# Products of w3 and w_out spread over steps 0 to 3 of a banded attention, and a feed-forward that begins with a whole pair of chunks

## Chip, core and metric

One core of one Trainium2 chip. The metric is the device time of one execution in microseconds (us). Engines: TensorE (PE; its weight loads are shown as PEld), VectorE (DVE), ScalarE (ACT), GpSimd (POOL, nearly unused here) and SyncE (SP), which issues all DMAs.

## The reference

Attention with a band of 96 keys and 8 global keys and a linear bias by distance, 4 batches, 8 heads, 768 tokens, head size 64; its output, as 3072 tokens by 512, goes through a gated feed-forward without a nonlinearity:

```python
scores = scale * np.matmul(q, k.transpose(0, 1, 3, 2)) + bias      # kept: 8 global keys, 96 local ones
a = softmax(np.where(keep, scores, -1e9))
x = np.matmul(a, v)            # 3072 x 512
a = x @ w1                     # 512 x 1024
b = x @ w2                     # 512 x 1024
h = a * b @ w3                 # 1024 x 1024
return h @ w_out               # 1024 x 512
```

The four weights are float64.

## The kernel before

**Attention in steps.** The tokens are cut into 12 chunks of 256. A step does two pairs of heads of one chunk, so a chunk takes 2 steps and there are 24. Step s has four parts. `visit(s)` does the products with v of step s - 1 on PE (L468), the scores of step s (L405), and, on ACT and DVE, the merging of the products with v into the chunk's x, which is split into a high and a low part, `xh` and `xl` (L503, L504, L63, L64). `all_rows(s)` adds the bias and takes the maximum on DVE (L420) and the exponential on ACT (L421). The scaling by the sums is on ACT (L433), from step 4 on half of it on DVE (L435). `turn(s, i)` transposes the probabilities of head pair i on PE (L445, L447), and ACT copies them out of PSUM as `ph` (L449). The transposes and the products with v share two PSUM buffers (pool `ps_v`).

**Feed-forward.** w3 and w_out are multiplied into one matrix first, so that the rest is (x w1 * x w2) (w3 w_out). `fold(f, k)` is one product of that, a float32 matmul of 128x128 by 128x512 (L142, two instructions in the trace), eight of them for each of eight blocks f of d_ff; after the eighth, ACT copies the block's high part `wh` out of PSUM (L144), and `low(f)` makes its low part on DVE (L147), which also frees the PSUM buffer. `run` is the feed-forward proper, with three matmuls for each product (high by high, high by low, low by high: L161 to L163, L178 to L180). For each f it makes `m` for w1 and for w2 in PSUM, copies the first to `a` (ACT, L168), multiplies on DVE (`g`, L171) and splits the result into `gh` and `gl`. The `m` tiles have two PSUM buffers, which folds use too. `run` works on 512 columns (a pair of chunks) or on 256 (one chunk). It yields after every 6 matmuls of 512 columns, or 12 of 256; `slices(k)` runs k of these pieces, and `SLICES` says how many go between the parts of a step. A pair is 48 pieces, 32 of products with w1 and w2 and 16 of output.

**Weights.** `weights` fetches a piece of float64 (512 KB) into a staging buffer by a DMA on SP's queue and makes float32 of it with three integer instructions on DVE (`convert`, L54, L56, L58). `w3(f)` does the two pieces of block f of w3, `w12(f)` the pieces of w1 and w2 of block f, which land in `t3s`; ACT then makes the high part (L122) and DVE, by `lows()`, the low one (L130). The staging buffers are four `stage` slots and two `raws` slots; a DMA into one waits until DVE has converted what was there.

**Order.** PE runs in the order of the program throughout. In `first_steps` DVE and SP do so as well, while ACT's instructions are put in order by a scheduler; later all engines but PE are scheduled, and ACT and DVE carry out their instructions in the order that results. `first_steps` interleaves the conversions, the 64 folds and the first steps of attention. In the kernel before it covers steps 0 to 3. Chunks 0 and 1 have feed-forwards of their own, of 256 columns, and that of chunk 0 begins in step 3.

## Time and profile before

| | |
|---|---|
| time, median of 3 runs | 591.76 us (591.63 to 592.16) |
| profiled execution: time, span | 591.84 us, 589.8 us |
| PE, DVE, ACT busy in the span | 565.4 us (96%), 274.2 us (46%), 297.3 us (50%) |
| mean granted clock of PE | 0.993 |

The span is the time from the first to the last instruction; the execution has 2.0 us more around it. "Busy" is the time in which an engine carried out at least one instruction. Matmuls overlap, so the distance between the starts of two of them is what one costs, and the duration of a single one is longer.

### The profile page before, as it was taken

To read this page: it belongs to the slowest core of one execution; us is meant where nothing else is said; L and a number is where in the kernel's file an instruction comes from. 1 tells how busy PE (TensorE), PEld (TensorE's weight loads), DVE (VectorE), ACT (ScalarE), POOL (GpSimd) and SP (SyncE) were. 2 spreads that over 40 slices of the span, in tenths; PEclk is the share of its full clock that TensorE was granted. 3 is DMA by queue.
4 is the path that set the end of the run, shared out by engine and by line. 5 is a ranking of instruction groups with operands and counts; after the bars stand their busy time and mean duration, and the time that the engine had idled before them with its cause. 6 is when DMAs were issued, how large, how long until landed. Compare 5 with 4: busy or idle time off the path is not lost.

```text
span 589.8 us, 12652 instructions
## 1 busy us (share of the span) xinstructions
PE 565.4 (96%) x5216; PEld 452.0 (77%) x5216; DVE 274.2 (46%) x875; ACT 297.3 (50%) x801; POOL 1.3 (0%) x10
## 2 busy tenths in 40 slices
PE   2998996999999999999999999999999999999995
PEld 0444556989988888888888888888888888888884
DVE  8999999524444445404534432552244354022200
ACT  3065688446666456536646545663555565322210
POOL 0000000000000000000000000000000000000000
PEclk9999997999999999999999999999999999999999
DMA  8896754202223202212210330221232020100001
GB/s 300 306 359 239 224 217 148 82 21 82 65 80 116 67 15 81 64 55 82 81 57 24 102 114 18 66 64 35 82 116 79 2 82 1 54 19 1 0 36 41
DMA packets 23252, 54.19 MB, mean 92 GB/s; under 512 B 2705, under 2 KB 4753, under 8 KB 23185
## 3 DMA queue, kind: packets, MB, share of 16 engines
q1 hardware_dynamic: 23184, 53.29, 26.6%
q8 instruction: 43, 0.70, 0.5%
q14 instruction: 25, 0.20, 0.1%
HBM read 46.99 MB, written 6.29 MB: 90 GB/s over the span
## 4 chain that ended last, share of the span: by engine, by line
PE 82%; DVE 13%; ACT 2%; DMA 2%; issue 1%; DVEq 0%; ACTq 0%
PE m L161 15%; PE m L162 15%; PE m L163 15%; PE o L178 8%; PE o L179 7%; PE o L180 7%; PE v L468 5%; PE s L405 4%; PE t L445 3%; PE t L447 3%; DVE pr L420 2%; DVE t L58 1%; DVE t L56 1%; DVE t3s L56 1%; DMA stage<-w3t 1%; DVE t3s L58 1%
## 5 line engine op out<-in xcount | busy, mean ns | idle before, releaser
L421 ACT ACTIVATE pr<-pr,mx 128x232 f32<-128x232 f32 (+1 forms) x192 | 88.3, 461 | 23.4 <-DVE mx L420 21.6
L171 DVE TENSOR_TENSOR g<-m,a 128x512 f32<-128x512 f32 x48 | 33.0, 687 | 132.0 <-PE m L163 128.6
L161 PE MATMUL m<-xh,w2h 128*128 128x512 f32 (+1 forms) x224 | 84.4, 377 | 0.0
L161 PE MATMUL m<-xh,w1h 128*128 128x512 f32 (+1 forms) x224 | 81.6, 364 | 0.0
L162 PE MATMUL m<-xl,w1h 128*128 128x512 f32 (+1 forms) x224 | 81.0, 362 | 0.0
L163 PE MATMUL m<-xh,w1l 128*128 128x512 f32 (+1 forms) x224 | 81.0, 361 | 0.0
L162 PE MATMUL m<-xl,w2h 128*128 128x512 f32 (+1 forms) x224 | 80.8, 361 | 0.0
L163 PE MATMUL m<-xh,w2l 128*128 128x512 f32 (+1 forms) x224 | 80.7, 360 | 0.0
L178 PE MATMUL o<-wh,gh 128*128 128x512 f32 x192 | 77.0, 401 | 0.0
L179 PE MATMUL o<-wl,gh 128*128 128x512 f32 x192 | 75.1, 391 | 0.0
L180 PE MATMUL o<-wh,gl 128*128 128x512 f32 x192 | 74.9, 390 | 0.0
L142 PE MATMUL w<-wo,t 128*128 128x512 f32 x128 | 60.6, 623 | 13.1 <-DVE wo L58 11.1
L449 ACT ACTIVATE ph<-t 128x512 f32<-128x512 f32 (+1 forms) x96 | 49.8, 557 | 44.2 <-PE t L447 29.5
L504 DVE TENSOR_TENSOR vs<-v,vs 128x512 f32<-128x512 f32 x24 | 16.6, 690 | 117.2 <-ACT vs L503 117.2
L63 ACT ACTIVATE gh<-g 128x512 fp32r<-128x512 f32 x48 | 30.3, 630 | 68.1 <-DVE g L171 68.1
L142 PEld LDWEIGHTS w<-wo,t 128*128 128x128 f32 x128 | 24.3, 198 | 42.5 <-issue 24.2
L420 DVE CUSTOM_DVE_ANT_0 pr<-s,biasw 128x232 f32<-128x232 f32 x160 | 54.9, 394 | 0.0
L168 ACT ACTIVATE a<-m 128x512 f32<-128x512 f32 x48 | 28.4, 591 | 45.0 <-PE m L163 45.0
L161 PEld LDWEIGHTS m<-xh,w2h 128*128 128x128 f32 x224 | 42.3, 189 | 8.7 <-issue 2.6
L161 PEld LDWEIGHTS m<-xh,w1h 128*128 128x128 f32 x224 | 43.0, 192 | 6.6 <-DVE t3s L58 0.2
L445 PE MATMUL t<-ident,pr 128*128 128x128 f32 x192 | 43.0, 278 | 5.3 <-ACT pr L433 5.2
L162 PEld LDWEIGHTS m<-xl,w1h 128*128 128x128 f32 x224 | 43.0, 192 | 6.4
(84 smaller groups left out, 800.5 us busy)
## 6 DMA issues: line engine op xcount, KB each, us to landing
qr<-qk SPq DMA_DIRECT2D x32, 312.0 KB, 4.4
vr<-vx SPq DMA_DIRECT2D x32, 256.0 KB, 3.5
stage<-w3t SPq DMA_DIRECT2D x15, 512.0 KB, 6.8
out_dram<-ot SPq DMA_DIRECT2D x24, 256.0 KB, 2.0
raws<-w SPq DMA_DIRECT2D x10, 512.0 KB, 6.1
qr<-qk SPq DMA_DIRECT2D x16, 260.0 KB, 4.1
vr<-vx SPq DMA_DIRECT2D x16, 192.0 KB, 3.7
stage<-w SPq DMA_DIRECT2D x6, 512.0 KB, 7.1
```

The costliest lines, as they stand in the source:

```text
L142: nc.tensor.matmul(ps, lhsT=self.t3[f, z][:, i * P:(i + 1) * P].bitcast(F32), rhs=self.wo[:, k].bitcast(F32), start=k == 0, stop=k == NFC - 1)
L161: nc.tensor.matmul(ps[:, z], lhsT=mh, rhs=xh[:, i], start=i == 0, stop=False)
L162: nc.tensor.matmul(ps[:, z], lhsT=mh, rhs=xl[:, i], start=False, stop=False)
L163: nc.tensor.matmul(ps[:, z], lhsT=ml, rhs=xh[:, i], start=False, stop=i == NCC - 1)
L171: nc.vector.tensor_tensor(out=g, in0=ps, in1=a, op=ALU.mult)
L178: nc.tensor.matmul(ps, lhsT=gh[:, f, ts], rhs=self.wh[:, f], start=f == 0, stop=False)
L179: nc.tensor.matmul(ps, lhsT=gh[:, f, ts], rhs=self.wl[:, f], start=False, stop=False)
L180: nc.tensor.matmul(ps, lhsT=gl[:, f, ts], rhs=self.wh[:, f], start=False, stop=f == NFC - 1)
L420: nc.vector.tensor_tensor_reduce(out=pr[:, j, u, w0:], in0=ps[u][:, j, w0:UW], in1=bias, scale=-SCALE, scalar=3.0e38, op0=ALU.add, op1=ALU ...
L421: nc.scalar.activation(pr[:, j, u, w0:], pr[:, j, u, w0:], AF.Exp, bias=m, scale=-1.0, accum_out=sm[:, j, u:u + 1])
L445: nc.tensor.transpose(pt[:, u, 0], pr[:, j, u, BW:UW], ident)
L449: nc.scalar.activation(ph[:, :, :nk], pt[:, :, :nk], AF.Copy)
```

## The change

The folds of blocks 3 to 7 are no longer done in one go between the parts of steps 0 to 2. `around` puts a few of them before, between and after the two turns of steps 0 to 3. `first_steps` covers step 4 too. The feed-forward of 256 columns is gone: the first `run` is that of chunks 0 and 1 together, it begins in step 4, after `visit(4)`, and gets 10 pieces there and 12 in each step after it. `low(2)` moves ahead of `w3(4)`. The conversions of w1 and w2 move back: block 0 comes as two single pieces after the rows of step 1, block 1 in step 2, blocks 2 and 3 in step 3, blocks 4 to 7 in step 4. Blocks 2, 4 and 5 go through `stage` slots, blocks 0, 1, 3, 6 and 7 through `raws` (before: 3, 5, 6 and 0, 1, 2, 4, 7). From step 8 on the program is the same; at its start both kernels have 46 of the first 48 pieces behind them.

```diff
--- before.py
+++ after.py
@@ -102,7 +102,7 @@
             if kind == "w":
                 f, n = divmod(at[0], 2)
 
-                raw = self.stage[{3: 0, 5: 2, 6: 0}[f] + n] if f in (3, 5, 6) else self.raws[:, n]
+                raw = self.stage[{2: 0, 4: 2, 5: 0}[f] + n] if f in (2, 4, 5) else self.raws[:, n]
                 dst, src = self.t3s[:, at[0] % 4], self.src[n][f]
                 fresh.append((n, f, dst.bitcast(F32).rearrange("p (i m) -> p i m", i=NCC)))
             elif kind == "o":
@@ -503,9 +503,7 @@
             nc.scalar.activation(v, uu[1], AF.Copy)
             nc.vector.tensor_tensor(out=v, in0=uu[0], in1=v, op=ALU.add)
             split(nc, *(x[:, h0:h0 + STEP] for x in xc), v)
-            if h0 + STEP == NP and c < 2:
-                work.append(ff.run(c, *xc, c * T, T))
-            elif h0 + STEP == NP and c % 2:
+            if h0 + STEP == NP and c % 2:
                 work.append(ff.run(c, *x2, (c - 1) * T, W))
         return ps
 
@@ -561,68 +559,75 @@
                 softmax(*p, *r, nc.scalar)
             loads(s + 1)
 
-        def fold_and_turn(f, s):
-            ff.fold(f, 0, 1, 2, 3)
-            turn(s, 0, prs)
-            ff.fold(f, 4, 5, 6)
-            turn(s, 1, prs)
-            ff.fold(f, 7)
+        def around(s, a, b, e):
+
+            for i, part in enumerate((a, b, e)):
+                for f, k0, k1 in part:
+                    ff.fold(f, *range(k0, k1 + 1))
+                if i < STEP:
+                    turn(s, i, prs)
 
         w3(3)
         scale(0)
         ff.low(0)
+        ff.low(2)
         w3(4)
         ff.low(1)
-        ff.low(2)
+        around(0, [(3, 0, 1)], [(3, 2, 2)], [(3, 3, 4)])
         w3(5)
-        w12(0)
-        fold_and_turn(3, 0)
+        prs = all_rows(1, visit(1))
+        ff.fold(3, 5, 6, 7)
+        ff.weights(("w", 0))
+        ff.low(3)
+        scale(1)
+        ff.weights(("w", 1))
+        around(1, [(4, 0, 4)], [(4, 5, 5)], [(4, 6, 7)])
         ff.lows()
         w3(6)
-        prs = all_rows(1, visit(1))
-        ff.low(3)
-        ff.fold(4, *range(NFC))
+        prs = all_rows(2, visit(2))
+        ff.low(4)
+        scale(2)
         w12(1)
-        scale(1)
-        ff.lows()
+        around(2, [(5, 0, 7), (6, 0, 0)], [(6, 1, 1)], [(6, 2, 3)])
+        ff.lows()
+        ff.low(5)
         w3(7)
-        ff.low(4)
-        fold_and_turn(5, 1)
         w12(2)
-        ff.lows()
-        ff.low(5)
-        prs = all_rows(2, visit(2))
-        ff.fold(6, *range(NFC))
+        prs = all_rows(3, visit(3))
+        ff.lows()
+        scale(3)
         w12(3)
-        scale(2)
+        around(3, [(6, 4, 7), (7, 0, 3)], [(7, 4, 5)], [(7, 6, 7)])
         ff.lows()
         ff.low(6)
-        fold_and_turn(7, 2)
         w12(4)
         ff.lows()
+        ff.low(7)
+        prs = all_rows(4, visit(4))
         w12(5)
-        ff.lows()
-        ff.low(7)
-        prs = all_rows(3, visit(3))
+        slices(2)
+        scale(4)
+        ff.lows()
+        slices(SLICES[0] - 2)
         w12(6)
+        turn(4, 0, prs)
         slices(2)
-        scale(3)
-        ff.lows()
+        ff.lows()
+        slices(SLICES[1] - 2)
         w12(7)
-        slices(SLICES[3][0] - 2)
-        ff.lows()
-        for i in range(STEP):
-            turn(3, i, prs)
-            slices(SLICES[3][i + 1])
+        turn(4, 1, prs)
+
+        slices(SLICES[2] - 2)
+        ff.lows()
         fits(nc, ff.mp, nf, oki)
 
 
-    SLICES = [()] * 3 + [(4, 4, 2)] * 3 + [(4, 2, 2)] * 2 + [(5, 4, 3)] * (n - 8)
+    SLICES = (5, 4, 3)
     with tc.manual_schedule(engines={mybir.EngineType.PE}):
         with tc.manual_schedule(engines={mybir.EngineType.DVE, mybir.EngineType.SP}):
             first_steps()
         with tc.manual_schedule(engines={mybir.EngineType.Activation}):
-            for s in range(4, n + 1):
+            for s in range(5, n + 1):
                 rs = all_rows(s, visit(s))
                 if s == n:
                     break
@@ -631,10 +636,10 @@
                 for p, r in zip(pairs(s), rs):
                     softmax(*p, *r, nc.vector)
                 loads(s + 1)
-                slices(SLICES[s][0] - 2)
+                slices(SLICES[0] - 2)
                 for i in range(STEP):
                     turn(s, i, rs)
-                    slices(SLICES[s][i + 1])
+                    slices(SLICES[i + 1])
             slices(10 ** 6)
```

Three places show what this does to the order. The names carry the head pair of the chunk and a buffer number. First, ACT in step 1. Before, its order after the exponentials of step 1 was:

```order
L144 ACTIVATE wh<-w_486 128x512
L122 ACTIVATE w1h<-t3s 128x512
L122 ACTIVATE w2h<-t3s 128x512
L433 ACTIVATE pr_2_463<-pr_2_463,sm_2_465 128x128 x2
L433 ACTIVATE pr_2_463<-pr_2_463,sm_2_465 128x232 x2
L433 ACTIVATE pr_3_474<-pr_3_474,sm_3_476 128x128 x2
L433 ACTIVATE pr_3_474<-pr_3_474,sm_3_476 128x232 x2
```

Now it is:

```order
L144 ACTIVATE wh<-w_340 128x512
L122 ACTIVATE w1h<-t3s 128x512
L433 ACTIVATE pr_2_437<-pr_2_437,sm_2_439 128x128 x2
L433 ACTIVATE pr_2_437<-pr_2_437,sm_2_439 128x232 x2
L433 ACTIVATE pr_3_448<-pr_3_448,sm_3_450 128x128 x2
L433 ACTIVATE pr_3_448<-pr_3_448,sm_3_450 128x232 x2
L449 ACTIVATE ph_2_0_504<-t_2_0_501 128x2x128
L449 ACTIVATE ph_2_1_511<-t_2_1_506 128x512
L449 ACTIVATE ph_3_0_517<-t_3_0_514 128x2x128
L449 ACTIVATE ph_3_1_524<-t_3_1_519 128x512
L122 ACTIVATE w2h<-t3s 128x512
L144 ACTIVATE wh<-w_495 128x512
```

The high part of w2's block, `w2h`, stood ahead of the scaling and now stands behind the copies of both turns.

Second, DVE around the conversion of the last block of w1 and w2. Before (the two rows at the top end that conversion, and the last row begins the merging of step 3's products with v):

```order
L56 SCALAR_TENSOR_TENSOR t3s<-raws,t3s 128x512 x2
L58 SCALAR_TENSOR_TENSOR t3s<-raws,t3s 128x512 x2
L171 TENSOR_TENSOR g_0_958<-m_0_1_933,a_0_899 128x512
L64 TENSOR_TENSOR gl_873<-g_0_958,gh_872 128x512
L130 TENSOR_TENSOR w1l<-t3s,w1h 128x512
L130 TENSOR_TENSOR w2l<-t3s,w2h 128x512
L171 TENSOR_TENSOR g_2_1030<-m_2_1_1005,a_2_1003 128x512
L64 TENSOR_TENSOR gl_873<-g_2_1030,gh_872 128x512
L319 TENSOR_SCALAR okt<-nf 128x1 x6
L320 TENSOR_REDUCE okt<-okt 128x1
L321 CAST oki<-okt 128x1
L504 TENSOR_TENSOR vs_2_1153<-v_1_2_1087,vs_2_1153 128x512
```

Now (from the split of the first `g` of step 4 to the merging of step 4's products with v):

```order
L64 TENSOR_TENSOR gl_1002<-g_0_1053,gh_1001 128x512
L54 TENSOR_SCALAR t3s<-raws 128x512 x2
L56 SCALAR_TENSOR_TENSOR t3s<-raws,t3s 128x512 x2
L58 SCALAR_TENSOR_TENSOR t3s<-raws,t3s 128x512 x2
L130 TENSOR_TENSOR w1l<-t3s,w1h 128x512
L130 TENSOR_TENSOR w2l<-t3s,w2h 128x512
L171 TENSOR_TENSOR g_1_1111<-m_1_1_1096,a_1_1094 128x512
L64 TENSOR_TENSOR gl_1002<-g_1_1111,gh_1001 128x512
L54 TENSOR_SCALAR t3s<-raws 128x512 x2
L56 SCALAR_TENSOR_TENSOR t3s<-raws,t3s 128x512 x2
L58 SCALAR_TENSOR_TENSOR t3s<-raws,t3s 128x512 x2
L504 TENSOR_TENSOR vs_0_1236<-v_2_0_1170,vs_0_1236 128x512
```

Blocks 6 and 7 now follow each other and both come through `raws`, and the merging that opens the next step's work stands straight behind block 7.

Third, SP's queue with the semaphores that each DMA waits for, at the last fetches of w1 and w2. Before:

```order
L383 DMA qr_0_913<-qk 128x624 [waits DMAHW7_49,PE_49]
L383 DMA qr_1_915<-qk 128x624 [waits DMAHW0_49,PE_49]
L390 DMA vr_0_917<-vx 128x512 [waits DMAHW1_49]
L390 DMA vr_1_919<-vx 128x512 [waits DMAHW2_49]
L50 DMA raws<-w 128x1024 [waits DMAHW3_49,DVE_49]
L50 DMA raws<-w 128x1024 [waits DMAHW4_49,DVE_49]
L390 DMA vr_2_1225<-vx 128x512 [waits DMAHW5_49,PE_49]
```

Now:

```order
L383 DMA qr_2_1030<-qk 128x624 [waits DMAHW1_49,PE_49]
L383 DMA qr_3_1032<-qk 128x624 [waits DMAHW2_49,PE_49]
L390 DMA vr_2_1034<-vx 128x512 [waits DMAHW3_49]
L390 DMA vr_3_1036<-vx 128x512 [waits DMAHW4_49]
L50 DMA raws<-w 128x1024 [waits DMAHW5_49,DVE_49]
L50 DMA raws<-w 128x1024 [waits DMAHW6_49,DVE_49]
L50 DMA raws<-w 128x1024 [waits DMAHW7_49,DMAHW5_49,DVE_49]
L50 DMA raws<-w 128x1024 [waits DMAHW6_49,DMAHW0_49,DVE_49]
L390 DMA vr_0_1296<-vx 128x384 [waits DMAHW1_49,PE_49]
```

The last two `raws` rows are block 7; their DVE semaphore is that of block 6's conversion, which empties the two slots.

## Rows read from the trace of the kernel before

**Rows 1.** The page: the busy time of each engine, and two rows of the span in 40 equal slices of 14.7 us (busy share in tenths; PEclk is the granted clock of TensorE in tenths of full speed).

```profile
PE 565.4 (96%) x5216; PEld 452.0 (77%) x5216; DVE 274.2 (46%) x875; ACT 297.3 (50%) x801; POOL 1.3 (0%) x10
...
PE   2998996999999999999999999999999999999995
...
PEclk9999997999999999999999999999999999999999
```

**Rows 2.** Windows of the span: stretch, its length, then busy us (and instructions) of PE, PEld, DVE, ACT, POOL; granted clock; DMA share; GB/s.

```profile
40.00:88.00 48.00, 45.84 (x436) 24.30 (x435) 45.62 (x115) 30.71 (x81) 0.00 (x0) 1.00 0.68 242
...
114.00:180.00 66.00, 65.96 (x786) 60.55 (x789) 28.70 (x116) 39.64 (x117) 0.00 (x0) 1.00 0.24 74
180.00:517.00 337.00, 337.00 (x3367) 279.20 (x3360) 131.96 (x481) 184.15 (x497) 0.00 (x0) 1.00 0.20 63
```

**Rows 3.** The waits of PE up to 130 us: line, waited for, us in total, times, longest. The first of them is that for the first weight.

```profile
PE w L142 <- DVE wo L58: 11.1, 1, 11.1
PE t L445 <- ACT pr L433: 5.2, 3, 4.7
PE w L142 <- DVE wl L147: 1.6, 1, 1.6
...
```

**Rows 4.** Timeline of step 3, engine by engine: start us, us, engine, line, what (a conversion and the reciprocal behind it on DVE, the high part of that weight and the scaling on ACT, the last matmul ahead of the wait and the first transpose on PE).

```profile
94.16 0.76 DVE L54 TENSOR_SCALAR t3s<-stage 128x512 int32<-128x512 int32 x2
...
97.24 0.16 DVE L426 TENSOR_SCALAR sm<-sm 128x4 f32<-128x4 f32 x1
...
96.76 0.63 ACT L122 ACTIVATE w1h<-t3s 128x512 fp32r<-128x512 f32 x1 [0.35 <-DVE t3s L58]
...
97.89 3.13 ACT L433 ACTIVATE pr<-pr,sm 128x232 f32<-128x232 f32 x8
...
93.47 0.28 PE L163 MATMUL m<-xh,w2l 128*128 128x256 f32 x1
98.42 0.47 PE L445 MATMUL t<-ident,pr 128*128 128x128 f32 x1 [4.67 <-ACT pr L433]
```

**Rows 5.** Windows around that wait, columns as in rows 2.

```profile
93.00:98.40 5.40, 0.75 (x7) 0.55 (x5) 5.33 (x20) 5.05 (x19) 0.00 (x0) 0.82 0.40 162
98.40:103.20 4.80, 4.78 (x23) 4.65 (x24) 4.34 (x9) 4.80 (x12) 0.00 (x0) 0.50 0.02 3
103.20:108.00 4.80, 4.80 (x42) 4.80 (x42) 2.33 (x4) 1.01 (x3) 0.00 (x0) 0.99 0.00 0
```

**Rows 6.** Timeline of PE: the folds of block 4 in step 1; 12 folds as 24 instructions; the first transpose of a turn and the fold behind it; products with v and scores of step 3 (the feed-forward follows at 87.73); two matmuls of 256 columns with 19 between them; two of 512 columns near the end with 18 between them.

```profile
47.75 7.13 PE L142 MATMUL w<-wo,t 128*128 128x512 f32 x16
...
68.49 10.57 PE L142 MATMUL w<-wo,t 128*128 128x512 f32 x24
...
83.20 0.27 PE L445 MATMUL t<-ident,pr 128*128 128x128 f32 x1
...
84.08 1.02 PE L142 MATMUL w<-wo,t 128*128 128x512 f32 x2
...
85.03 1.63 PE L468 MATMUL v<-ph,vr 64*64 64x64 f32 x96
86.48 1.32 PE L405 MATMUL s<-qr 64*64 64x168 f32 x32
...
88.19 0.28 PE L161 MATMUL m<-xh,w1h 128*128 128x256 f32 x1
...
90.59 0.28 PE L163 MATMUL m<-xh,w1l 128*128 128x256 f32 x1
...
579.10 0.39 PE L179 MATMUL o<-wl,gh 128*128 128x512 f32 x1
...
583.40 0.39 PE L180 MATMUL o<-wh,gl 128*128 128x512 f32 x1
```

**Rows 7.** Timeline of step 2, DVE and ACT: merging, the first of the eight rows and the work behind them on DVE; the first exponential and the last read of a sum, and copies of a turn with a high part behind them on ACT.

```profile
69.93 0.68 DVE L504 TENSOR_TENSOR vs<-v,vs 128x512 f32<-128x512 f32 x1
...
71.92 0.39 DVE L420 CUSTOM_DVE_ANT_0 pr<-s,biasw 128x232 f32<-128x232 f32 x1
...
74.47 0.76 DVE L54 TENSOR_SCALAR t3s<-stage 128x512 int32<-128x512 int32 x2
...
72.35 0.49 ACT L421 ACTIVATE pr<-pr,mx 128x232 f32<-128x232 f32 x1 [1.08 <-DVE mx L420]
...
76.05 0.19 ACT L421 ACTIVATION_READ_ACCUMULATOR pr<-pr,mx 128x1 f32 x1
...
81.72 1.06 ACT L449 ACTIVATE ph<-t 128x512 f32<-128x512 f32 x2
82.68 0.62 ACT L122 ACTIVATE w1h<-t3s 128x512 fp32r<-128x512 f32 x1
```

**Rows 8.** Timeline of ACT and DVE: the high part of block 2; the low part of block 0 and the next instruction.

```profile
37.27 0.58 ACT L144 ACTIVATE wh<-w 128x512 fp32r<-128x512 f32 x1
...
35.22 0.66 DVE L147 TENSOR_TENSOR wl<-w,wh 128x512 fp32r<-128x512 f32 x1
35.80 0.42 DVE L54 TENSOR_SCALAR t<-stage 128x512 int32<-128x512 int32 x1
```

**Rows 9.** The `raws` slots: the last issue of a pair of fetches on SP, and the time from issue to landing of all ten.

```profile
89.36 0.85 SPq L50 DMA_DIRECT2D raws<-w  x2
...
DMA to landing us min/median/max: 3.6/6.1/8.8
```

More of the change, by code (lines that the diff above doesn't have):

```diff
@@ L573, in first_steps @@
         ff.low(0)
+        ff.low(2)
         w3(4)
         ff.low(1)
-        ff.low(2)
+        around(0, [(3, 0, 1)], [(3, 2, 2)], [(3, 3, 4)])
         w3(5)
-        w12(0)
-        fold_and_turn(3, 0)
+        prs = all_rows(1, visit(1))
[5 more added lines that the diff above has]
+        around(1, [(4, 0, 4)], [(4, 5, 5)], [(4, 6, 7)])
         ff.lows()
         w3(6)
-        prs = all_rows(1, visit(1))
-        ff.low(3)
-        ff.fold(4, *range(NFC))
+        prs = all_rows(2, visit(2))
+        ff.low(4)
+        scale(2)
         w12(1)
-        scale(1)
-        ff.lows()
-        w3(7)
-        ff.low(4)
-        fold_and_turn(5, 1)
-        w12(2)
+        around(2, [(5, 0, 7), (6, 0, 0)], [(6, 1, 1)], [(6, 2, 3)])
         ff.lows()
         ff.low(5)
-        prs = all_rows(2, visit(2))
-        ff.fold(6, *range(NFC))
+        w3(7)
+        w12(2)
+        prs = all_rows(3, visit(3))
+        ff.lows()
+        scale(3)
         w12(3)
-        scale(2)
+        around(3, [(6, 4, 7), (7, 0, 3)], [(7, 4, 5)], [(7, 6, 7)])
         ff.lows()
         ff.low(6)
-        fold_and_turn(7, 2)
         w12(4)
         ff.lows()
+        ff.low(7)
+        prs = all_rows(4, visit(4))
         w12(5)
+        slices(2)
+        scale(4)
         ff.lows()
-        ff.low(7)
-        prs = all_rows(3, visit(3))
+        slices(SLICES[0] - 2)
         w12(6)
+        turn(4, 0, prs)
         slices(2)
-        scale(3)
         ff.lows()
+        slices(SLICES[1] - 2)
         w12(7)
-        slices(SLICES[3][0] - 2)
+        turn(4, 1, prs)
+        slices(SLICES[2] - 2)
         ff.lows()
-        for i in range(STEP):
-            turn(3, i, prs)
-            slices(SLICES[3][i + 1])
         fits(nc, ff.mp, nf, oki)
-    SLICES = [()] * 3 + [(4, 4, 2)] * 3 + [(4, 2, 2)] * 2 + [(5, 4, 3)] * (n - 8)
+    SLICES = (5, 4, 3)
     with tc.manual_schedule(engines={mybir.EngineType.PE}):
```

## Prediction

> **What bounds the kernel now.** I read the page first: PE is busy for 96% of the span, and the slices in which it is not are the first, the seventh and the last [rows 1]. The windows by stage say where each engine stands: from 114 us to the end of attention PE never stops, while up to 88 us it is DVE that is full, 45.6 of 48 us, with conversions of weights [rows 2]. So a change of the opening counts in two ways: by PE's work, and by the places where PE stands because DVE or ACT is late. The waits name those: 5.2 us for scaled probabilities, nearly all of it in one wait of 4.7 us, and 1.6 us for a low part that frees a buffer [rows 3]. The timeline of that wait shows the pattern that decides this change. DVE converts weights from 94.16 to 97.24, only then comes the reciprocal, ACT makes the high parts of those weights first, scales from 97.89, and PE, idle since 93.6, starts at 98.42, half a microsecond after the scaling [rows 4]. The wait costs more than itself: the granted clock falls during it and is 0.50 (1.2 instead of 2.4 GHz) for 4.8 us behind it [rows 5]. 4.8 us at half the clock are 2.4 us lost, of which I count 2.2, since the transposes among that work go at ACT's pace anyway.
>
> **What is removed.** Feed-forwards of 256 columns have 2 x 8 x 2 x 4 x 3 = 384 matmuls; as 512 columns they are 192. Twenty of 256 columns take 2.40 us, 0.120 each; nineteen of 512 take 4.30 us, 0.226 each [rows 6]. 384 x 0.120 - 192 x 0.226 = 46.1 - 43.5 = 2.6 us less on PE, all of it on the path. The Trainium skill (TensorE: Matmul & The Clock Gate, section Back-to-back issue gap) has a matmul cost its columns at 2.4 GHz and 2.5 ns, 0.109 and 0.216 us; by that the gain would be 0.5 us, and the forecast 2.1 us longer. The trace measures these very shapes and decides.
>
> Of before's waits, 6.8 us and the 2.2 us of slow clock go, since those places no longer exist: 9.0 us. The question is what stands in the new places. Conversions, folds, steps and pieces up to the start of step 8 are the same in number, so the difference is settled there.
>
> **The new waits, worked forward.** Units from the rows: a conversion of two pieces 3.1 us (97.24 - 94.16) [rows 4]; merging to rows 2.0, eight rows 2.55, their exponentials from 0.4 behind the first row for 3.9, a copy of a turn 0.48 [rows 7]; a fold (two instructions) 0.88, a turn 0.88, products with v 1.45, scores 1.25 [rows 6]; a piece of feed-forward is 6 x 0.226 = 1.35; a low part and a high part 0.6 each [rows 8].
>
> *Step 1.* Until 35.8 us nothing differs. Then `low(2)` needs a high part that ACT makes at 37.27 to 37.85 [rows 8], so DVE stands for 2.1 us and `w3(4)`, `low(1)` and `w3(5)` end at 45.3. Merging, rows 1 and their exponentials follow to 51.0; wh(3), `low(3)`, the reciprocals: scaling starts at 52.6. PE began its folds behind the scores of step 1 at 47.75 [rows 6]; with three folds fewer ahead of that it begins at 45.1, is through 8 of them at 52.1 and can start the turn at 53.1, half a microsecond behind the scaling: 1.0 us. The second turn needs PSUM that the copies behind the scaling free: 0.5 more. The high part of w2's block 0 stands behind all four copies on ACT, until 57.9; DVE, in order, waits 2.9 us for it ahead of `w3(6)`.
>
> *Step 2.* That puts rows 2 at 63.6 and their exponentials to 67.9. PE (second turn from 55.8, two folds, visit 2 until 60.9, nine folds) comes at 68.8 and finds the first turn ready. The second needs `ph` of the first copied, behind the scaling (8 x 0.39) and wh(5): 72.05 against 70.6, 1.4 us. The high parts of block 1 are set between the copies, so DVE stands 2.3 us again, and `low(5)` ends at 75.3.
>
> *Step 3.* `w3(7)` and `w12(2)`, 6.2 us, bring DVE to 81.4; ACT does both high parts of that block before it splits x; rows 3 run from 83.9, the exponentials to 88.2, wh(6), scaling from 88.6. PE (turn, two folds, visit 3 by 77.4, eight folds) is there at 84.4 and gets its turn at 89.2: 4.7 us, as long as before's. I take the same fall of the clock, 2.2 us: 6.9.
>
> *Start of the feed-forward.* At half clock the turn and two folds last until 94.2; another turn and two folds, and block 7 is done near 96.8; wh(7) and both high parts of block 4 precede the merging on ACT, `low(7)` on DVE: x is whole at 101.8. PE is there after visit 4, at 99.5, but the first 6 matmuls read head pairs that are ready: 0.8 us.
>
> *Step 4.* `m` of block 1 needs the buffer that `a_0` frees, behind the exponentials (to 106.0): 1.0 us. The turn needs rows 4 (to 104.3), `w12(5)` (107.4), the high parts of block 5, scaling from 108.6, at 109.2 against 108.0: 1.2, and 0.4 because the turn, until 110.6, goes at the pace of the scaling: 2.6 in all.
>
> *Step 5.* ACT scales until 111.7, then gh_0; DVE splits it, 113.0, and converts block 6 until 116.0; both high parts of it on ACT, both low ones, g_1, gh_1 and the split keep DVE until 120.0. Block 7 comes next, and SP may fetch it into `raws` only from 116.0; before, its fetch was issued at 89.36, far ahead. A fetch landed after 3.6 us at the least, 6.1 in the median, among others [rows 9]; the second is issued about 0.45 later, so 4.05 to 6.5. One step's keys and values were fetched long before, so the queue is empty and I take 4.7, nearer the least: 120.7, of which 0.7 lies open. [...] Block 7 is then converted at 123.5. Queued behind it on DVE are the merging of step 4, two low parts, the check of `fits`, the low part of x, rows 5 and last `g_2`: 0.6 + 1.3 + 0.5 + 0.9 + 2.6 + 0.65, 6.6 us: 130.1. PE meanwhile does four pieces, a turn and one piece until 118.2, visit 5 and four pieces until 126.4, and then needs the `m` buffer that `g_2` reads: 3.7 us. A wait of that length takes the clock down too, as the 4.7 did: 2.2. Together 5.9.
>
> **Sum.** 1.5 + 1.4 + 6.9 + 0.8 + 2.6 + 5.9 = 19.1 us of new waits, against 9.0 + 2.6 = 11.6 saved: 7.5 us longer. On the profiled execution's 591.84 (0.08 above the median, 591.76) that is **599.3 us**. Bounds: the fetch between 4.05 and 6.5 puts the last wait between 3.0 and 5.5. The clock behind it is unknown: 3.0 us may not take it down, so 0 to 2.2. The chain through steps 1 to 3 has some twenty hand-overs of 0.03 to 0.1 us, each perhaps 0.05 off: 1 us either way. Together 595.5 to 602.
>
> **Rivals.** *Step 5 has no wait.* Then 5.9 goes: 593.4, still slower. For it: only steps of 0.6 us make up the chain on ACT and DVE, and PE has 8 us of work after visit 5's start. Against: DVE reaches block 7 at 120.0 even with its fetch hidden, which saves 0.7 of the 3.7; the rest hangs on the merging standing behind that conversion, and the order has it there.
>
> *DVE is not late in step 3.* This one decides the sign. If the waits of DVE for ACT (2.1 + 2.9 + 2.3 = 7.3 us) are not there, or shorter by 4.7 in all, scaling in step 3 starts by 83.9, PE never stands and the clock stays: minus 6.9, 592.4, which is 0.1% from before. For it: ACT's order was made by a scheduler, and ACT was busy only 30.7 of 48 us [rows 2]. Against: its queue is in order, and in the order now w2h of block 0 stands behind four copies. Without step 5's wait too: 586.5.
>
> *The change does not do what it says:* if PE had the same places of waiting as before, only the 2.6 us would move: 589.2. Against: every place named has another neighbour now.
>
> The Trainium skill (TensorE: Matmul & The Clock Gate, section The HAM clock gate) says an idle array loses half its clock until it has worked again; rows 5 show that after 4.7 us. That it would fall after each of the two long waits is taken into the sum; if it falls in neither, 594.9.
>
> **How the numbers follow.** Forecast, both long waits: 0.63 (595.5 to 602). More than that: 0.07. No wait in step 5: 0.10 (593.4, spread 1.5). DVE not late in step 3: 0.10 (592.4, spread 1.5). Both, or only the 2.6 us: 0.10 (586 to 589). A measurement here can tell 0.2%, 1.2 us, from no change: slower is above 593.0. From the cases: 0.63 + 0.07 + 0.06 + 0.04 = 0.80 slower; 0.04 + 0.05 = 0.09 same; 0.11 faster. The range reaches to the two cases around 593 and leaves out the fastest and the slowest: 592.3 to 602.
>
> **What would show it.** In the changed kernel's trace: no matmul of 256 columns; a wait of PE for scaled probabilities of 4 to 5 us near 89 us, with the clock at 0.50 behind it; a second long wait, for `g`, near 126 to 130 us, with block 7's fetch issued near 116 and converted near 123.5; w2h of block 0 near 57 us with DVE idle ahead of `w3(6)`. From the start of step 8 the two run alike, 7 us apart. The prediction is wrong if PE is full from 84 us on, or if `g_2` ends before 126 us.

## The result, and the profile after

The changed kernel takes 596.0 us (median of 5, 595.2 to 597.8) where the kernel before took 591.7 in the same comparison: a ratio of 1.0075, with an interval of 1.0062 to 1.0088. It is slower by 4.4 us; 7.5 had been forecast, and the range was 592.3 to 602.

The page of the changed kernel, its busy times and two rows of slices of 14.8 us:

```profile
PE 564.9 (95%) x5024; PEld 440.6 (74%) x5024; DVE 273.7 (46%) x871; ACT 299.4 (50%) x805; POOL 1.3 (0%) x10
...
PE   2999979989999999999999999999999999999995
...
PEclk9999999989999999999999999999999999999998
```

PE is busy half a microsecond less than before and the span is 3.6 us longer [rows 1], so on balance what was lost is idle time. The slices show where: one dip in the sixth, where the kernel before had one in the seventh, and another in the ninth, with a lower clock. The waits of PE up to 200 us name the causes (waited for, us in total, times, longest):

```profile
PE w L142 <- DVE wo L58: 11.2, 1, 11.2
PE t L445 <- ACT pr L433: 5.5, 4, 3.9
PE m L161 <- DVE g L171: 2.7, 1, 2.7
PE t L445 <- ACT ph L449: 1.5, 2, 1.2
PE m L161 <- ACT a L168: 0.6, 1, 0.6
PE w L142 <- DVE t L58: 0.4, 1, 0.4
PE m L162 <- DVE xl L64: 0.2, 1, 0.2
```

The first line is the wait for the first weight, as before [rows 3]. The rest stands in these places (timeline of PE: start, duration, and in brackets the idle time ahead of the instruction and who ended it; 97.88 and 104.14 are the first and the last matmul of the first block of the feed-forward):

```profile
52.63 1.00 PE L445 MATMUL t<-ident,pr 128*128 128x128 f32 x3 [1.04 <-ACT pr L433]
...
71.65 0.33 PE L445 MATMUL t<-ident,pr 128*128 128x128 f32 x1 [1.18 <-ACT ph L449]
...
88.21 0.47 PE L445 MATMUL t<-ident,pr 128*128 128x128 f32 x1 [3.94 <-ACT pr L433]
...
97.88 0.50 PE L161 MATMUL m<-xh,w1h 128*128 128x512 f32 x1
...
100.37 0.50 PE L162 MATMUL m<-xl,w1h 128*128 128x512 f32 x1 [0.23 <-DVE xl L64]
...
104.14 0.39 PE L163 MATMUL m<-xh,w2l 128*128 128x512 f32 x1
105.09 0.50 PE L161 MATMUL m<-xh,w1h 128*128 128x512 f32 x1 [0.57 <-ACT a L168]
...
127.43 0.50 PE L161 MATMUL m<-xh,w2h 128*128 128x512 f32 x1 [2.67 <-DVE g L171]
```

Every place of the forecast is there: step 1, the second turn of step 2, the turn of step 3, the start of the feed-forward, `m` of block 1 (the row at 105.09), and `g_2` in step 5 (the product `g` of block 2, counted from 0). Behind the two long waits the granted clock is at its lower level (columns as in [rows 2]):

```profile
88.00:91.50 3.50, 3.29 (x10) 2.30 (x11) 2.90 (x7) 3.50 (x10) 0.00 (x0) 0.51 0.63 256
...
129.00:132.40 3.40, 3.23 (x13) 2.86 (x13) 1.23 (x4) 2.90 (x7) 0.00 (x0) 0.50 0.00 0
```

What makes the scaling of step 3 late is on DVE, where the idle time in brackets is time in which no weight was converted (low part of block 2; on ACT the high part of w2's block 0 and on DVE the low part that waited for it; second piece of block 1; first row of step 3; low part of the x of chunk 1):

```profile
37.37 0.69 DVE L147 TENSOR_TENSOR wl<-w,wh 128x512 fp32r<-128x512 f32 x1 [1.37 <-ACT wh L144]
...
56.96 0.62 ACT L122 ACTIVATE w2h<-t3s 128x512 fp32r<-128x512 f32 x1
...
57.62 0.69 DVE L130 TENSOR_TENSOR w2l<-t3s,w2h 128x512 fp32r<-128x512 f32 x1 [2.68 <-ACT w2h L122]
...
69.12 0.43 DVE L54 TENSOR_SCALAR t3s<-raws 128x512 int32<-128x512 int32 x1 [0.79 <-DMA raws<-w]
...
82.98 0.39 DVE L420 CUSTOM_DVE_ANT_0 pr<-s,biasw 128x232 f32<-128x232 f32 x1
...
99.62 0.69 DVE L64 TENSOR_TENSOR xl<-vs,xh 128x512 fp32r<-128x512 f32 x1 [0.70 <-ACT xh L63]
```

### The profile page after: what moved, and what is told of

Its sections match the earlier page's. It is cut to its first block, busy times and chain, and to the rows that moved or that the text cites. A ratio compares the mean times of both kernels' runs of the same rounds, so it can differ in the third digit from the quotient of the medians.

```text
span 593.4 us, 12270 instructions
## 1 busy us (share of the span) xinstructions
PE 564.9 (95%) x5024; PEld 440.6 (74%) x5024; DVE 273.7 (46%) x871; ACT 299.4 (50%) x805; POOL 1.3 (0%) x10
## 4 chain that ended last, share of the span: by engine, by line
PE 79%; DVE 12%; ACT 6%; DMA 1%; issue 1%; DVEq 0%; ACTq 0%
PE m L161 14%; PE m L162 14%; PE m L163 14%; PE o L178 8%; PE o L179 7%; PE o L180 7%; PE v L468 5%; PE t L445 3%; PE s L405 3%; PE t L447 3%; ACT pr L421 2%; ACT pr L433 2%; DVE t L56 2%; DVE t L58 2%; DVE pr L420 1%; DVE t L54 1%
## 5 line engine op out<-in xcount | busy, mean ns | idle before, releaser
L161 PE MATMUL m<-xh,w2h 128*128 128x512 f32 x192 | 79.3, 413 | 2.7 <-DVE g L171 2.7
L161 PE MATMUL m<-xh,w1h 128*128 128x512 f32 x192 | 75.3, 392 | 0.7 <-ACT a L168 0.6
L162 PE MATMUL m<-xl,w2h 128*128 128x512 f32 x192 | 75.5, 393 | 0.0
L163 PE MATMUL m<-xh,w2l 128*128 128x512 f32 x192 | 75.4, 393 | 0.0
L162 PE MATMUL m<-xl,w1h 128*128 128x512 f32 x192 | 74.9, 390 | 0.2 <-DVE xl L64 0.2
L163 PE MATMUL m<-xh,w1l 128*128 128x512 f32 x192 | 74.8, 390 | 0.0
L445 PE MATMUL t<-ident,pr 128*128 128x128 f32 x192 | 44.2, 283 | 7.0 <-ACT pr L433 5.5
L64 DVE TENSOR_TENSOR gl<-g,gh 128x512 fp32r<-128x512 f32 x48 | 33.2, 691 | 28.5 <-ACT gh L63 28.1
L161 PEld LDWEIGHTS m<-xh,w2h 128*128 128x128 f32 x192 | 36.4, 190 | 12.6 <-DVE g L171 3.1
L433 ACT ACTIVATE pr<-pr,sm 128x232 f32<-128x232 f32 (+1 forms) x116 | 44.8, 461 | 0.7 <-DVE sm L426 0.6
```

What stands on the lines that cost most here:

```text
L161: nc.tensor.matmul(ps[:, z], lhsT=mh, rhs=xh[:, i], start=i == 0, stop=False)
L162: nc.tensor.matmul(ps[:, z], lhsT=mh, rhs=xl[:, i], start=False, stop=False)
L163: nc.tensor.matmul(ps[:, z], lhsT=ml, rhs=xh[:, i], start=False, stop=i == NCC - 1)
L433: nc.scalar.activation(x, x, AF.Copy, scale=r)
L445: nc.tensor.transpose(pt[:, u, 0], pr[:, j, u, BW:UW], ident)
```

## The experiments

Two explanations were open. Either each wait of PE has its own cause and goes when that is removed, or DVE's whole work up to some point is the bound, and its order only decides where PE stands; in the first three expectations below, the second is theory A. All ratios below are to the kernel before; a thousandth is 0.6 us. Diffs are against the changed kernel unless said otherwise.

**A wait of DVE taken away.**

```diff
         around(1, [(4, 0, 4)], [(4, 5, 5)], [(4, 6, 7)])
-        ff.lows()
         w3(6)
```

> One line less than the changed kernel: the low part of w2's block 0, for which VectorE stood 2.68 us at 57.6 us, is made behind the conversion of w3's block 6 instead of ahead of it. Theory A (VectorE's idle time is what PE later stands for, but the next thing is late at once): VectorE gains 2.7 us up to rows 2, step 2's wait of 1.18 us at the second turn goes, and then VectorE stands for block 1 of w1 and w2, whose fetch SP issues at 62.05 only because it is queued behind the keys of step 3: that wait of 0.79 us grows to 3 to 3.5 us, PE's turn of step 3 stays near 88 us, and the time is within 0.5 us of the changed kernel: ratio to before 1.0065 to 1.008. Rival B (a wait of VectorE that is taken away is time won): rows 3 come 2.7 us earlier, step 3's wait shrinks from 3.94 to 1.3 us: 4 us less with the clock, ratio 1.001.

Measured: 1.0073 (1.0054 to 1.0092), as the changed kernel. The wait of 2.68 us is gone, the wait of PE in step 2 shrinks from 1.18 to 0.31, and the turn of step 3 comes at 87.81, 0.4 us sooner; these 0.4 us stand again at `g_2`, where PE waits 3.06 us instead of 2.67. The rest is eaten by the next thing, as theory A had it, and by less than it had: 1.9 us (0.8 in the changed kernel) for two fetches, issued behind the keys of step 3 (SP's issues, then DVE).

```profile
60.18 0.90 SPq L383 DMA_DIRECT2D qr<-qk  x2
61.13 0.90 SPq L390 DMA_DIRECT2D vr<-vx  x2
62.12 0.85 SPq L50 DMA_DIRECT2D raws<-w  x2
...
60.28 0.69 DVE L504 TENSOR_TENSOR vs<-v,vs 128x512 f32<-128x512 f32 x1 [1.80 <-ACT vs L503]
...
68.01 0.43 DVE L54 TENSOR_SCALAR t3s<-raws 128x512 int32<-128x512 int32 x1 [1.00 <-DMA raws<-w]
69.29 0.43 DVE L54 TENSOR_SCALAR t3s<-raws 128x512 int32<-128x512 int32 x1 [0.86 <-DMA raws<-w]
```

The other 1.8 us stand in the fourth line: DVE now comes to the merging of step 2 before PE has made those products.

**The same, with the fetch sooner.**

```diff
         scale(2)          # without loads(3)
         w12(1)
+        loads(3)
```

> As the run before, and the fetch of block 1 of w1 and w2 is issued ahead of the keys and values of step 3 instead of behind them. Theory A: now the 2.7 us and some of the waits for block 1 are won (0.8 for the fetch): rows 3 come about 3.7 us earlier, step 2's wait of 1.18 is gone, step 3's is 1 to 1.5 us instead of 3.94 and the clock does not fall there; at the start of the feed-forward VectorE is behind PE by 1 to 2 us. Together 2.5 to 5 us less than the changed kernel, likeliest 3.8: ratio to before 1.001. The wait and the clock of step 5 (2.67 us, 0.50 behind it) stay. Rival B: the fetch decides nothing, this and the run before are the same to 0.5 us.

Measured: 1.0070 (1.0053 to 1.0087): nothing is won, against 3.8 us forecast. Up to step 3 the theory holds in part. The fetches of block 1 cost no wait, PE waits 1.66 us for the turn of step 3 instead of 3.94, and the clock stays at 1.00 there. But the second turn of step 2 still waits, for 1.43 us, and the rows of step 3 come 2.2 us sooner and not 3.7, since DVE stands 1.73 and 0.58 us for products that PE has not made yet. And the feed-forward now waits:

```profile
86.00 0.33 PE L445 MATMUL t<-ident,pr 128*128 128x128 f32 x1 [1.66 <-ACT pr L433]
...
99.20 0.51 PE L161 MATMUL m<-xh,w1h 128*128 128x512 f32 x1 [2.92 <-ACT xh L63]
```

2.9 us, and the fall of the clock that belonged to step 3 is behind that wait instead. Ahead of x stand, on DVE, the conversions of blocks 3 and 4 and the low parts of 6 and 7. DVE came to them 2 us sooner, stood 2.1 us among them for the fetch of block 3 and for high parts (0.6 in the changed kernel), and x was whole only 0.4 us sooner.

**Only the order of DVE changed.**

```diff
         w3(7)
-        w12(2)
         prs = all_rows(3, visit(3))
-        ff.lows()
         scale(3)
+        w12(2)
         w12(3)
```

> In the changed kernel, the conversion of block 2 of w1 and w2 (3.1 us of VectorE) moves from ahead of the rows of step 3 to behind their reciprocals. Theory A (VectorE's whole work up to the feed-forward is the bound, so its order there decides only where PE stands): scaling of step 3 starts near 84.6 us, PE's wait of 3.94 us shrinks to under 1 us and the clock stays up at 88 us; but x is whole no earlier than 100 us, so PE stands 4 to 5 us at the start of the feed-forward, with the clock low behind that. Time within 1 us of the changed kernel: ratio 1.006 to 1.009. Rival B (the wait in step 3 is a matter of place and goes with the conversion): 3.1 + 1.6 us less, ratio 1.000.

Measured: 1.0102 (1.0087 to 1.0116), 1.6 us over the changed kernel. The wait in step 3 is 0.39, and PE stands 1.77 us for a low part, which frees a buffer of `m`, and 4.66 us at the start of the feed-forward (timeline of PE; the granted clock is 0.54 in the 3.6 us behind the second of them):

```profile
95.93 0.50 PE L161 MATMUL m<-xh,w1h 128*128 128x512 f32 x1 [1.77 <-DVE wl L147]
...
102.25 0.80 PE L161 MATMUL m<-xh,w1h 128*128 128x512 f32 x1 [4.66 <-ACT xh L63]
...
85.65 0.43 DVE L54 TENSOR_SCALAR t3s<-stage 128x512 int32<-128x512 int32 x1 [0.99 <-DMA stage<-w]
86.95 0.43 DVE L54 TENSOR_SCALAR t3s<-stage 128x512 int32<-128x512 int32 x1 [0.88 <-DMA stage<-w]
```

The wait has moved, as theory A says; x is even later, because block 2's fetch now stands behind the keys of step 4 on SP (the last two rows, DVE). So up to the start of the feed-forward what counts is how much work, and how much waiting, stands on DVE ahead of x, and in these three kernels neither another order nor one wait less within it helps.

**Block 7 taken out of step 5.** The merging of step 4's products is split in two, since the x of chunk 2 takes the memory of `t3s` and `raws`: the sum `v` is made at once and its split waits until block 7 is done. With this step 5 belongs to `first_steps`, so there too DVE and SP follow the order of the program and ACT's order is the scheduler's; behind `first_steps` it is the other way round (there kernel.py puts ACT in the order of the program and leaves DVE and SP to the scheduler; the section on order has ACT scheduled there too).

```diff
-        w12(7)
         turn(4, 1, prs)
         slices(SLICES[2] - 2)
         ff.lows()
+        prs = all_rows(5, visit(5, late))   # without the split
+        slices(2)                           # g_2
+        ...                                 # scaling of step 5
+        w12(7)
+        ...                                 # loads(6), 3 pieces, turn(5, 0), a piece
+        ff.lows()
+        split(nc, *(x[:, 0:STEP, 0:T] for x in xs[1]), late[0])
```

> In the changed kernel, the conversion of block 7 of w1 and w2 and the low parts behind it move from ahead of the rows of step 5 to behind g_2 and the scaling of step 5 (the split of x for chunk 2 goes behind them, since it takes their buffers). Theory A: behind 127 us VectorE has time to spare, so this wait does go: m_3_1 needs no wait (2.67 us), the turn of step 5 none, the clock stays up at 129 us (1.6 us): 4.3 us less than the changed kernel, ratio to before 1.000 (0.9985 to 1.002). Rival B (VectorE is still behind, the wait moves to g_3 or to the turns of step 5): less than 1.5 us, ratio over 1.005.

Measured: 0.9985 (0.9976 to 0.9995), 591.5 us, 5.3 us less than the changed kernel by the ratios, 4.6 by the medians, and a little faster than the kernel before. `g_2` starts at 123.07 instead of 126.69, no wait of PE is left behind 108.06, and the clock is at 1.00 where the changed kernel has 0.50:

```profile
129.00:132.40 3.40, 3.40 (x16) 2.81 (x15) 2.70 (x5) 2.43 (x5) 0.00 (x0) 1.00 0.01 2
...
126.00:140.00 14.00, 14.00 (x169) 11.73 (x172) 9.85 (x28) 8.46 (x16) 0.00 (x0) 1.00 0.01 2
```

So the wait of step 5 was a cost of its own, and the time gives back at least what the trace of the changed kernel shows there, 2.67 and 0.17 us of waits and 1.7 of slow clock: behind the start of the feed-forward DVE has time to spare (9.85 us busy of 14, the second row).

**What 256 columns cost where PE never stands.**

```diff
-            if h0 + STEP == NP and c % 2:
+            if h0 + STEP == NP and c in (4, 5):
+                work.append(ff.run(c, *xc, c * T, T))
+            elif h0 + STEP == NP and c % 2:
```

> The changed kernel with chunks 4 and 5 fed forward in 256 columns each instead of 512 together, in a stage where PE never stands: 384 matmuls of 256 columns for 192 of 512. By the pitches of the trace (0.120 and 0.226 us) 2.6 us longer than the changed kernel: ratio to before 1.0119, between 1.010 and 1.0135. By the rule of the Trainium skill (TensorE: Matmul & The Clock Gate, section Back-to-back issue gap; columns at 2.4 GHz and 2.5 ns) 0.5 us longer: ratio 1.0083. In the trace the stretch from 180 us to the last visit is longer by the same amount, with PE full.

Measured: 1.0122 (1.0101 to 1.0144), 2.8 us over the changed kernel. In the traces, from the first transpose of step 5's second turn to the last matmul, PE full in both, it is 451.96 us against 449.76, 2.2 more. The pitch is that of [rows 6]: from the second row to the third, 12 matmuls, are 1.44 us (the last two rows are the changed kernel's).

```profile
135.99 0.27 PE L445 MATMUL t<-ident,pr 128*128 128x128 f32 x1
...
272.64 0.28 PE L161 MATMUL m<-xh,w1h 128*128 128x256 f32 x1
...
274.08 0.28 PE L161 MATMUL m<-xh,w1h 128*128 128x256 f32 x1
...
587.95 0.39 PE L180 MATMUL o<-wh,gl 128*128 128x512 f32 x1
...
137.12 0.27 PE L445 MATMUL t<-ident,pr 128*128 128x128 f32 x1
...
586.88 0.39 PE L180 MATMUL o<-wh,gl 128*128 128x512 f32 x1
```

By the traces the term of 2.6 us is right to 0.4, and 0.5 us, the estimate by the isolated gap in the Trainium skill (TensorE: Matmul & The Clock Gate, section Back-to-back issue gap), is not what happens here.

**Blocks 4 to 7 later, without and with the changes of steps 1 to 3.** Block 4 goes behind the rows of step 4, 5 (through `raws` now) ahead of its first turn, 6 behind the scaling of step 5, 7 behind `g_4`. The first kernel below has that alone, the second also the low part and the fetch from above (and `loads(4)` behind `w12(3)`), the third also block 2 behind the reciprocals; these are the changes of steps 1 to 3. All have the split of `v` late and step 5 in `first_steps`, as in the kernel with block 7 alone.

```diff
         ff.low(6)
-        w12(4)
-        ff.lows()
         ff.low(7)
         prs = all_rows(4, visit(4))
-        w12(5)
+        w12(4)
         ...
-        w12(6)
+        w12(5)
         turn(4, 0, prs)
```

> The run before without the low part and the fetches: only the conversions of blocks 4 to 7 one place later. Theory A: step 3's wait of 3.9 us and its fall of the clock stand as in the changed kernel, since all that moved lies behind it; the step-5 wait is gone: ratio to before 0.9975, within 0.1% of the kernel with block 7 alone moved. Rival B (VectorE's whole work does it, wherever it is taken away): as the run before, 0.992.

> Together: the low part and the fetch of the second experiment, the fetch of block 3 of w1 and w2 ahead of the keys of step 4, and the conversions of blocks 4 to 7 each one place later than in the changed kernel (4 behind the rows of step 4, 5 ahead of its first turn, 6 behind the scaling of step 5, 7 behind g_4). Theory A (what counts is how much of VectorE's work stands ahead of the start of the feed-forward, since behind it VectorE has time to spare): x of chunk 1 is whole near 95 us instead of 100, so the 2.9 us that the second experiment lost there come back; step 3's wait stays 1.7 us with no fall of the clock; no wait for g in step 5: 587.5, ratio to before 0.992 (0.990 to 0.995). Rival B (VectorE stays behind through step 5, the waits come back as waits for g or for scaled probabilities in steps 4 and 5): ratio over 0.997.

> As the one with all three, and block 2 converted behind the reciprocals of step 3, as in the third experiment. Theory A: PE's turn of step 3 comes without a wait (1.7 us less there), but x of chunk 1 is no earlier than in the kernel with all three (near 95 us), so PE waits 1 to 2 us at the start of the feed-forward instead: the same time to 0.5 us, ratio 0.992. Rival B (the wait in step 3 was all): 1.7 us less, 0.989.

Measured, in this order: 1.0101 (1.0085 to 1.0116), 1.0073 (1.0059 to 1.0087) and 1.0041 (1.0027 to 1.0055); all three miss by a wait that nothing had foreseen. In the third (timeline of PE and of ACT, then a window behind it):

```profile
138.90 2.73 PE L468 MATMUL v<-ph,vr 40*64 40x64 f32 x91 [5.75 <-ACT ph L449]
...
138.25 0.60 ACT L449 ACTIVATE ph<-t 128x512 f32<-128x512 f32 x1 [0.76 <-DVE xl L64]
```

```profile
138.90:143.00 4.10, 4.10 (x124) 4.10 (x126) 0.64 (x2) 0.60 (x1) 0.00 (x0) 0.50 0.20 65
```

The sum `v` that waits for its split lies in one of the four buffers that the copies of a turn use. With block 7 converted some 5 us later than in the kernel with block 7 alone, the fourth copy of step 5 could not start until the split had read it, and the products of step 6 stood behind the copy. Apart from that steps 1 to 3 go as theory A says, or better: in the third kernel PE does not wait for the scaling of step 3, nor at the start of the feed-forward (1 to 2 us expected; 2.9 in the kernel with the low part and the fetch alone).

**The tile, and block 7 ahead of `g_4`.** The third kernel again, with `v` in the tile of the output, which nothing else uses by then:

```diff
-            v = at.tile([P, STEP, T], F32, tag="ph", bufs=4, name=f"vs_{c}_{h0}")
+            v = ff.mp.tile([P, STEP, T], F32, tag="o", name=f"vs_{c}_{h0}")   # in step 5
         ...
         turn(5, 0, prs)
         slices(1)
         ff.lows()
+        w12(7)
         ...
         turn(5, 1, prs)
         slices(1)                           # g_4
-        w12(7)
```

> As the kernel with all three and block 2 behind the reciprocals, but the sum of the products of step 4 that waits for its split lies in a tile of its own kind (that of the output) instead of in one of the four that the copies of the turns use, and block 7 is converted ahead of g_4 instead of behind it. Theory A (the 5.75 us in which PE stood for a copy at 138.9 us, and the slow clock behind it, come from that tile alone: the fourth copy of step 5 waited until the split had read it, behind the conversion): both go, PE is full from 103 us on: against the changed kernel 4.5 us less up to 100 us and 4.4 us less in step 5, 587.1 in all, ratio to before 0.992 (0.990 to 0.994). Rival B (VectorE is still behind in step 6, whatever the tile): waits for g or for scaled probabilities between 135 and 150 us of 2 us or more, ratio over 0.995.

> As the run before, but block 7 is still converted behind g_4 (132 to 138 us). Theory A: the 5.75 us for the copy go, but the merging of step 6 stands behind that conversion on VectorE, rows of step 6 run from 139.5 to 142, so PE waits about 2 us for the turn of step 6 or for g_5: 589 to 591, ratio 0.995 to 0.998. Rival B (the tile was all): as the run before to 0.5 us.

> The first of these without the changes of steps 1 to 3 (low part, fetches, block 2): blocks 4 to 7 later, and the tile. Theory A: the wait of 3.9 us in step 3 and its fall of the clock stay, everything behind is clean: ratio 0.9975 (0.996 to 0.999), the same as block 7 alone, and 3.5 us or 0.6% over the run with all. Rival B (what is saved ahead of the feed-forward is lost behind it): the same as that run.

Measured: 587.6 us, 0.9933 (0.9920 to 0.9946), for the first; 0.9942 (0.9929 to 0.9955) with block 7 still behind `g_4`; 1.0008 (0.9999 to 1.0017) without the changes of steps 1 to 3. The waits of PE in the first, up to 260 us, and two of its windows:

```profile
PE w L142 <- DVE wo L58: 11.3, 1, 11.3
PE t L445 <- ACT ph L449: 3.2, 3, 1.4
PE t L445 <- ACT pr L433: 1.3, 2, 1.0
PE m L161 <- DVE g L171: 0.6, 1, 0.6
...
```

```profile
84.00:98.00 14.00, 12.57 (x170) 8.56 (x169) 13.07 (x34) 10.72 (x27) 0.00 (x0) 1.00 0.28 92
...
126.00:140.00 14.00, 14.00 (x183) 11.59 (x182) 11.31 (x33) 7.29 (x17) 0.00 (x0) 1.00 0.40 137
```

Behind the first weight no wait of PE is longer than 1.43 us, and the clock is up from 50 to 520 us. This version beats both kernels: by 8.4 us the changed one, by 3.9 the one before. The tile was worth 5.9 us (1.0041 against 0.9942, with nothing else changed). Where block 7 stands is worth 0.5 (0.9942 against 0.9933), which the intervals do not tell from nothing: here rival B was right, and theory A had 2 us for a wait for `g` that was 0.9. And the changes of steps 1 to 3 are worth 4.4 us (1.0008 against 0.9933), since with only the later blocks the scaling of step 3 is still waited for, for 4.2 us, and the clock falls. That kernel was expected to equal the one with block 7 alone and is 1.4 us over it; its trace has a wait of 0.98 us for a `g` near 147 us, which the other has not, and its turn of step 3 comes 0.7 us later, but neither was tested.

**One half of the change alone.** The kernel before with chunks 0 and 1 in 512 columns, in its own order:

```diff
-            if h0 + STEP == NP and c < 2:
-                work.append(ff.run(c, *xc, c * T, T))
-            elif h0 + STEP == NP and c % 2:
+            if h0 + STEP == NP and c % 2:
```

> One part of the change alone: the kernel before, in its own order, with chunks 0 and 1 fed forward together in 512 columns. Theory A (the narrow feed-forward of chunk 0 was the work under which VectorE converted; without it PE has none from visit 3 on): the four pieces between 87.7 and 93.5 us go, PE stands from 87.7 to 98.4 us for the scaling of step 3, 10.7 instead of 4.7 us, and the six pieces around the turns go too, so visit 4 comes near 101 us and the feed-forward starts at 104 to 106, against 97.9 in the changed kernel; no wait behind that, since VectorE is through. 5.5 us of the changed kernel's later waits and slow clock are saved, 6 to 9 are lost: 596 to 599.5, likeliest 598, ratio 1.0105. So the order of the changed kernel is worth 2 us of what the wide feed-forward costs at the start. Rival B (the wide feed-forward is worth its 2.6 us wherever it starts): 589, ratio 0.9955.

Measured: 1.0137 (1.0120 to 1.0155), 8.1 us over the kernel before and just past what was expected. PE stands where the four pieces were, its clock falls while it stands and stays low behind it, and the feed-forward starts at 108.25 (104 to 106 expected):

```profile
98.05 0.47 PE L445 MATMUL t<-ident,pr 128*128 128x128 f32 x1 [10.61 <-ACT pr L433]
```

```profile
98.00:105.50 7.50, 6.07 (x79) 4.94 (x83) 5.74 (x18) 5.73 (x13) 0.00 (x0) 0.50 0.00 0
```

So what the change loses is the feed-forward of chunk 0, which began at 87.73 and was the work under which DVE converted. The rest of the change, the new order, wins back 3.7 of those 8.1 us.

## Why the prediction was right, and where it was off

*The sign and the mechanism* were right: DVE is late where it waits for high parts that ACT makes late and for fetches, so the scaling of step 3 is, and block 7 in front of the rows of step 5 makes `g_2` late. The places and times agree: w2h at 56.96 (57 forecast), the turn of step 3 at 88.21 (89.2), the matmul that needs `g_2` at 127.43 (130.1). From step 8 on the two kernels run alike, 3.5 us apart (7 forecast).

*The sizes* were nearly all too high. Waits: step 1 1.36 (1.5 forecast), step 2 1.18 (1.4), step 3 3.94 (4.7), start of the feed-forward 0.23 (0.8), step 4 0.87 (2.2, and 0.4 for the pace of the scaling), step 5 2.84 (3.7); 10.4 us together, where 14.7 had been summed without the clock. The turn of step 4 took 0.46 us more than one of 0.88, as forecast (0.4), which the list of waits does not hold. Nor does it hold all of the start of the feed-forward: a wait is counted there from the end of the last matmul as the profile draws it (0.39 us, not its pitch of 0.226), and by their starts the 24 matmuls from 97.88 to 104.14 take 6.26 us where 23 pitches of 0.226 are 5.20, so 1.06 us were lost and the forecast of 0.8 was about right. The largest miss is in step 4: `a_0` came at 104.47 instead of 106.0 and the scaling at 106.53 instead of 108.6, because DVE was through with x at 100.3 instead of 101.8. In step 5 the fetch made DVE stand for 0.75 us, as forecast (0.7), and the same lead of 1 to 2 us made the wait shorter. The chain through steps 1 to 3 had been worked out 1.0 us too late at the turn of step 3, which is the 1 us of the bounds. On the way there DVE stood 5.8 us for ACT and fetches where 7.3 had been forecast for ACT alone: 1.4 for the low part of block 2 (2.1 forecast), 2.7 for that of w2's block 0 (2.9), and 1.8 at block 1 (2.3), of which 0.8 was a fetch that the prediction did not have there.

*The clock.* Each fall lasted 3.4 us in the profiled execution, so it cost 1.7 us and not 2.2; in another kernel, behind the same wait, it lasted longer (last section).

*What these leave.* By its own trace the changed kernel should then be 10.4 + 0.5 + 3.4 - 9.0 - 2.6 = 2.7 us longer; the two profiled spans are 3.6 apart. The other 0.9 us were not assigned; the 0.8 us that the start of the feed-forward lost beyond its listed 0.23 would be most of it. The medians are 4.4 apart: the profiled execution of the changed kernel, 595.2, is the shortest of its five. So the measured 596.0 us lies near the low end of the bounds of the sum, 595.5 to 602, because nearly every term of it was too high.

*The rivals.* That DVE is not late in step 3 is refuted by its waits, and that only the 2.6 us would move, by the new places. That step 5 has no wait is refuted by the trace, and the kernel with block 7 taken out of it shows what that rival would have been worth: 591.5, where 593.4 had been worked out. What the prediction did not see is that its two large terms differ in kind: the second goes when its cause is moved, the first only moves to the start of the feed-forward as long as the same conversions stand ahead of x (1.0070 and 1.0102 in the kernels that try it).

## What to carry to other kernels

A wait on the bounding engine names who was last, not what has to be taken away: behind an engine that converts and computes in order, ask up to which point all of its work is due, and move work past that point rather than within it. Here it took both halves: fewer waits ahead of the point gained nothing alone (1.0070), work moved past it gained nothing over moving block 7 alone (1.0008 against 0.9985), and together they gave 0.9933. Narrow matmuls that cost 2 to 3 us more on PE can be the cheaper choice if they let it start 10 us sooner under another engine's work. Before a transfer or a split is put off, look at what shares its queue and its buffers: here a fetch stood behind keys that waited for PE, and one tile that was held for a late split cost nearly 6 us.

## What the runs showed of the hardware

The granted clock does not answer to the length of a wait alone. After waits of 1.8 us or less it stayed up in every trace; after 2.67, 2.76, 2.86, 2.92 and 3.06 us it fell; after 2.91 us in the kernel with narrow chunks 4 and 5 it did not, although that part of the program is the changed kernel's, and there the fall had come after 2.67. And after the same wait of 3.94 us it was low for 3.4 us in the changed kernel and for longer in the one with block 7 taken out (first the kernel with narrow chunks, behind its wait; then the one with block 7 taken out, behind the turn of step 3, where the changed kernel has 1.00):

```profile
129.50:133.00 3.50, 3.42 (x19) 3.00 (x20) 1.74 (x5) 2.83 (x8) 0.00 (x0) 1.00 0.00 0
```

```profile
91.50:95.00 3.50, 3.50 (x13) 1.94 (x12) 3.50 (x7) 2.17 (x5) 0.00 (x0) 0.70 0.00 0
```

This cost the second kernel 1.0 us: its feed-forward began at 98.89, the changed kernel's at 97.88. The Trainium skill (TensorE: Matmul & The Clock Gate, section The HAM clock gate) has an idle array lose half its clock until it has worked again; the traces agree, and show besides that which of the shorter waits does it differs from one execution to the next: the five executions of the changed kernel had mean granted clocks from 0.985 to 0.996. Their times lie within 2.6 us of each other, those of the version that has no long wait within 0.8; but those of the third kernel with the later blocks, which has a wait of 5.75 us, lie within 0.6, so a long wait by itself need not widen the spread.
